# Layer norm and MLP on one core: which of two DMA queues loads the second tile of x

## The chip, the cores and the metric

The kernel runs on one core of a Trainium2 chip. The metric is the device time of one execution in microseconds (us); of several runs the median is given. TensorE is PE in the profile (PEld is its weight load), VectorE is DVE, ScalarE is ACT, GpSimd is POOL, and SyncE is SP. SPq and ACTq are the instructions with which SP and ACT hand a DMA to their queue.

## What is computed

```python
B, S, D, F = 1, 2048, 1024, 3584          # all tensors bf16

def reference(x, w1, b1, w2, b2):
    y = _layernorm(x, axis=-1)            # (x - mean) / sqrt(var + 1e-5), no scale, no shift
    h = _gelu(jnp.einsum("bsd,df->bsf", y, w1) + b1)   # tanh form
    return jnp.einsum("bsf,fd->bsd", h, w2) + b2
```

## The kernel before

**Tiles and blocks.** The 2048 tokens are 16 tiles of 128 (x0, x1, ...), and four tiles make a block of 512. For each block a first product makes 28 rows of h (each 128 features by 512 tokens, eight matmuls over the 1024 input features, L330) and ScalarE applies gelu to each (L350). A second product (L379) takes the block's h times w2, VectorE adds b2 (L390), and SP stores. All weights stay on the chip once loaded, so the loads lie at the start: about 19 MB in the first 60 us, while PE already multiplies.

**The opening.** Block 0 is special, because PE can't wait for four normalised tiles and a whole w1. Tiles 0, 1 and 2 go in as centred but unscaled values (c_sb). Tile 0: ScalarE sums the first half of each row (L400), VectorE the second half (L402), and VectorE subtracts both sums in two pieces (L407). Tiles 1 and 2: `raw_tile` adds the two halves and sums them (L412), then writes 1024*x minus the sum (L416). PE transposes each tile (pe_T, L304) and ScalarE copies the result to yT_sb (L310). The missing scale is multiplied in later, at the first rows of h (L347). Until data are there, PE runs matmuls on a constant (`fill`, L290), 37 of them ahead of tile 0's transposes and two within them.

**The order of PE's work** in the opening is written out by hand. OPEN (L22) lists steps: (0, 0, 2) is tile 0 with the input features 0 to 255, for the first four rows of h (8 matmuls of 128 columns); (1, None) is the transposes of tile 1; and so on:

```python
OPEN = ((0, 0, 2), (1, None), (0, 2, 4), (0, 4, 6), (1, 0, 6), (0, 6, 8), (2, None), (1, 6, 8), (2, 0, 8))
```

PE takes its instructions in this order. A step that isn't ready holds up all steps behind it.

**The pieces of w1** (`w1_chunks`, L111). The first four cover columns 0 to 511 (four rows of h) with 256 input features each, 256 KB apiece. In this text they are called w1 pieces 0 to 3. Piece 0 serves (0, 0, 2), piece 1 (0, 2, 4), piece 2 (0, 4, 6) and the first use of (1, 0, 6) beyond pieces 0 and 1, piece 3 (0, 6, 8). Pieces 4 and 5 cover columns 512 to 767, and four larger pieces follow.

**The order of the loads** (L200 to L220) is the order in which SP and ACT issue them. Each issue is a `dma_start` in the program of the engine whose queue it uses, by way of the helper `dma` (L177, recorded at L178). Tiles 0 and 1 are loaded in halves of 512 columns (128 KB each): the first half by SP, the second by ACT. Then SP alone issues w1 pieces 0, 1, 2, tile 2, piece 3, tile 3, pieces 4 and 5, b1, the rest of w1, block 1 of x, w2, b2 and the last blocks of x. After its two issues ACT runs the table load for gelu (L399) and the sum for tile 0 (L400).

**Waits.** Every DMA has a semaphore of its own. L400 waits for the first half of tile 0, L402 for its second half, L412 for both halves of tile 1 (L421) or for tile 2 (L424). The first matmul that uses a w1 piece waits for that piece, and pe_T waits for the centred tile.

VectorE's other work in the opening (bn_stats of the tiles at L231 for the scale, and the normalisation of tile 3 at L245) stands in a list by hand as well (L421 to L435). Later VectorE work is placed by a planner with estimated times (L521 to L536); it takes those for loads from the running sum of bytes in `dma` and so doesn't know the queue.

## Time and profile before

| | us |
|---|---|
| median of three runs | 398.07 |
| lowest and highest of them | 397.82, 398.11 |
| the profiled execution | 398.39 |
| span of its trace | 397.2 |
| PE busy in that span | 392.3 (99%) |
| DVE, ACT, POOL busy | 156.6, 82.7, 9.5 |

The span runs from the first instruction to the last; the remaining 1.2 us of the profiled execution lie around it. Each time inside the trace counts from the start of the span. "Busy" for PE includes matmuls that wait in the pipeline. The view of waits lists for how long an engine stood idle and what released it; the chain is followed back from the last instruction to what released each step.

| when each load was issued and when its data were there | queue | issued | landed |
|---|---|---|---|
| x0, first half | SP | 0.79 | 3.5 |
| x0, second half | ACT | 0.78 | 3.7 |
| x1, first half | SP | 1.22 | 4.3 |
| x1, second half | ACT | 1.22 | 4.6 |
| w1 piece 0 | SP | 1.69 | 6.36 |
| w1 piece 1 | SP | 2.16 | 7.28 |
| w1 piece 2 | SP | 2.67 | 7.96 |
| x2 | SP | 3.18 | 8.65 |
| w1 piece 3 | SP | 3.69 | 9.39 |

The issue times are the timeline's, the landings the trace's: a load comes down in 16 parts, each of which is recorded, and has landed with the last.

### The profile page before, as it was taken

The page shows a single profiled execution, that of the slowest core. Times are in us where ns is not written, and L with a number is a line of the kernel's source. Part 1 is how long each engine was busy: PE and PEld are TensorE (multiplying, and loading weights), DVE is VectorE, ACT ScalarE, POOL GpSimd, SP SyncE. Part 2 cuts the span into 40 slices and gives each one's busy share as a digit, 9 for nine tenths or more (in the row PEclk, how much of TensorE's full clock was granted, in tenths as well). Part 3 has the DMA queues.
Part 4 walks back from the last instruction along what each step waited for, and adds up shares of the span by engine and source line. Part 5 has one row for each costly group of instructions (what it writes and reads, how often), then busy time and mean ns, then how long its engine had stood idle before and what let it go on. Part 6 is the DMA issues. An engine that isn't in the chain of part 4 may idle for free.

```text
span 397.2 us, 4608 instructions
## 1 busy us (share of the span) xinstructions
PE 392.3 (99%) x1968; PEld 187.9 (47%) x2003; DVE 156.6 (39%) x341; ACT 82.7 (21%) x125; POOL 9.5 (2%) x25
## 2 busy tenths in 40 slices
PE   8999999999999999999999999999999999999998
PEld 8844444444444444444444444444444444444445
DVE  4957889988999405988100000001100000001011
ACT  4264430000134442000024433100003334400000
POOL 0201100011000100000000000000000000000000
DMA  8999940000000000000000000000000000000000
GB/s 257 353 386 386 387 164 15 26 26 16 26 1 2 0 0 2 27 15 26 26 15 0 0 2 0 11 17 26 15 26 13 2 0 0 2 13 26 15 26 26
DMA packets 17357, 23.62 MB, mean 59 GB/s; under 512 B 1082, under 2 KB 9786, under 8 KB 17338
## 3 DMA queue, kind: packets, MB, share of 16 engines
q1 hardware_dynamic: 17050, 23.08, 16.7%
q8 instruction: 15, 0.25, 0.3%
q10 hardware_dynamic: 288, 0.26, 0.2%
q14 instruction: 4, 0.03, 0.0%
HBM read 19.14 MB, written 4.19 MB: 59 GB/s over the span
## 4 chain that ended last, share of the span: by engine, by line
PE 97%; DMA 1%; issue 1%; SPq 0%; DVE 0%
PE ps L379 49%; PE ps L330 48%; DMA w_sb<-in_w_dram 1%; SPq L178 0%; PE ps L304 0%; DVE o_sb L390 0%
## 5 line engine op out<-in xcount | busy, mean ns | idle before, releaser
L330 PE MATMUL ps<-yT_sb,w_sb 128*128 128x512 bf16 (+2 forms) x989 | 193.9, 355 | 1.2
L379 PE MATMUL ps<-w_sb,hT_sb 128*128 128x512 bf16 (+2 forms) x908 | 193.3, 373 | 0.8
L330 PEld LDWEIGHTS ps<-yT_sb,w_sb 128*128 128x128 bf16 x1008 | 92.5, 98 | 101.4 <-DMA w_sb<-in_w_dram 0.6
L379 PEld LDWEIGHTS ps<-w_sb,hT_sb 128*128 128x128 bf16 x924 | 89.2, 98 | 104.5
L350 ACT ACTIVATE hT_sb<-ps,b_sb 128x512 bf16<-128x512 f32 x112 | 76.2, 688 | 255.9 <-PE ps L330 231.8
L390 DVE TENSOR_TENSOR o_sb<-ps,b_sb 128x512 bf16<-128x512 f32 (+2 forms) x33 | 22.3, 675 | 198.9 <-PE ps L379 198.8
L277 DVE STREAM_TRANSPOSE yT_sb<-x_sb 32x256 bf16<-32x256 bf16 x192 | 83.7, 436 | 21.6 <-PE ps L330 18.6
L231 DVE BATCH_NORM_STATS2 st_sb<-x_sb 128x6 f32<-128x512 bf16 x32 | 20.9, 668 | 0.1
L347 DVE TENSOR_TENSOR ps<-ps,rbc_sb 128x384 f32<-128x384 f32 x28 | 15.2, 563 | 9.4 <-PE ps L330 9.0
L235 POOL TENSOR_TENSOR rstd_sb<-mv_sb,nhalf 128x1 f32<-128x1 f32 x16 | 8.7, 549 | 124.2 <-DVE mv_sb L238 124.1
L245 DVE TENSOR_SCALAR x_sb<-x_sb,mv_sb,rstd_sb 128x1024 bf16<-128x1024 bf16 x13 | 7.1, 545 | 2.8 <-POOL rstd_sb L235 2.0
L310 ACT COPY yT_sb<-ps 128x384 bf16<-128x384 bf16 (+2 forms) x10 | 4.5, 504 | 6.8 <-PE ps L304 6.8
L290 PE MATMUL ps<-const-bfloat16-1.0 128*128 128x128 bf16 x39 | 4.5, 310 | 0.8 <-PEq L565 0.8
L290 PEld LDWEIGHTS ps<-const-bfloat16-1.0 128*128 128x128 bf16 x39 | 4.1, 145 | 0.8 <-issue 0.8
L238 DVE BATCH_NORM_AGGREGATE mv_sb<-st_sb 128x2 f32<-128x15 f32 x16 | 3.5, 217 | 0.8
L304 PE MATMUL ps<-ident,c_sb 128*128 128x128 bf16 x24 | 2.4, 249 | 0.1
L402 DVE TENSOR_SCALAR_CACHE_REDUCE junk_d<-x_sb 128x512 bf16<-128x512 bf16 x1 | 0.7, 686 | 3.7 <-DMA x_sb<-in_x_dram 3.7
L304 PEld LDWEIGHTS ps<-ident,c_sb 128*128 128x128 bf16 x24 | 1.8, 111 | 0.3 <-issue 0.3
L412 DVE SCALAR_TENSOR_TENSOR junk_d<-x_sb 128x512 bf16<-128x512 bf16 x2 | 1.4, 688 | 1.1 <-DMA x_sb<-in_x_dram 1.1
L399 ACT ACT_TABLE_LOAD x1 | 1.3, 1283 | 1.7 <-PEq L565 1.7
L446 DVE STREAM_TRANSPOSE rbc_sb<-rs_sb 32x96 f32<-32x96 f32 x4 | 1.1, 270 | 0.1
L416 DVE TENSOR_SCALAR c_sb<-x_sb,sum_sb 128x1024 bf16<-128x1024 bf16 x2 | 1.0, 487 | 0.1
(22 smaller groups left out, 6.8 us busy)
## 6 DMA issues: line engine op xcount, KB each, us to landing
w_sb<-in_w_dram SPq DMA_DIRECT2D x4, 1792.0 KB, 18.5
w_sb<-in_w_dram SPq DMA_DIRECT2D x2, 2048.0 KB, 14.4
out_dram<-o_sb SPq DMA_DIRECT2D x31, 128.0 KB, 1.7
x_sb<-in_x_dram SPq DMA_DIRECT2D x3, 1024.0 KB, 14.5
w_sb<-in_w_dram SPq DMA_DIRECT2D x6, 256.0 KB, 5.5
w_sb<-in_w_dram SPq DMA_DIRECT2D x1, 1024.0 KB, 9.3
x_sb<-in_x_dram SPq DMA_DIRECT2D x2, 256.0 KB, 5.7
w_sb<-in_w_dram SPq DMA_DIRECT2D x1, 512.0 KB, 6.4
```

The source lines that it names most:

```text
L231: return (lambda e, i=i, h=h: e.bn_stats(st_sb[:, i, 6 * h:6 * (h + 1)], x_sb[:, i, h * HC:(h + 1) * HC]), [x_ev.get(i, f"x{i}_{h}")], f"s ...
L235: pool.op(lambda e, i=i: e.tensor_tensor(out=rstd_sb[:, i:i + 1], in0=mv_sb[:, i, 1:2], in1=nhalf[:, i:i + 1], op=ALU.pow), waits=[f"mv{i} ...
L245: return (lambda e, i=i: e.tensor_scalar(out=x_sb[:, i, :], in0=x_sb[:, i, :], scalar1=mv_sb[:, i, 0:1], scalar2=rstd_sb[:, i:i + 1], op0= ...
L277: res.append((lambda e, src=src, dst=dst: e.transpose(out=dst, in_=src), waits, (f"tr{i}" if lastop else None), 0.47))
L290: pe.op(lambda e: e.matmul(ps[:, 0, 0:P], lhsT=one, rhs=one, start=True, stop=True), waits=[gate] if gate else [])
L304: pe.op(lambda e, j=j, o=(j - j0) * P: e.transpose(out=bap[:, o:o + P], in_=src[:, j * P:(j + 1) * P], identity=ident[:, :]), waits=waits, ...
L310: act.op(lambda e, dst=dst, psrc=psrc: e.copy(out=dst, in_=psrc), waits=[f"tp{i}_{j0}"], sig=f"te{i}_{j0}")
L330: pe.op(lambda e, b=b, r=r, dt=dt, n0=n0, n1=n1, bank=bank: e.matmul(ps[:, bank, n0:n1], lhsT=w1_sb[:, dt, r * P:(r + 1) * P], rhs=yT_sb[: ...
L347: crit.append((est[sig], (lambda e, bank=bank: e.tensor_tensor(out=ps[:, bank, 0:n], in0=ps[:, bank, 0:n], in1=rb, op=ALU.mult), [sig, "rb ...
L350: act.op(lambda e, r=r, bank=bank: e.activation(out=hT_sb[:, r, :], in_=ps[:, bank, :], func=ACT.Gelu_apprx_tanh, bias=b1_sb[:, r:r + 1], ...
L379: pe.op(lambda e, st=st, ft=ft, c0=c0, c1=c1, bank=bank: e.matmul(ps[:, bank, 0:c1 - c0], lhsT=hT_sb[:, ft, st * P:(st + 1) * P], rhs=w2_s ...
L390: crit.append((est[sig], (lambda e, ob=ob, c0=c0, c1=c1, bank=bank: e.tensor_tensor(out=o_sb[:, ob, c0:c1], in0=ps[:, bank, 0:c1 - c0], in ...
```

## The change

The loop that loads the first two tiles takes SP's queue for the first half of tile 0 alone. The first half of tile 1 goes to ACT's queue.

```diff
         for i in range(2):
-            for h, q in enumerate((sp, act)):
+            for h, q in enumerate((sp if i == 0 else act, act)):
                 dma(x_sb[:, i, h * HC:(h + 1) * HC], xf[i * P:(i + 1) * P, h * HC:(h + 1) * HC],
                     f"x{i}_{h}", P * HC * 2, q)
         for ci in range(3):
             load_w1(ci)
```

SP's program then begins with the first half of x0, w1 pieces 0, 1, 2, x2, and so on. ACT's begins with the second half of x0, the first half of x1, the second half of x1, the table load. No transfer, wait, semaphore or computation is added or removed.

## The prediction

> **What bounds the kernel now.** I read the page's busy line first, then the chain in order of time, then the waits of the first 20 us, then the timeline from 3.5 to 8 us.

> ```profile
> PE 392.3 (99%) x1968; PEld 187.9 (47%) x2003; DVE 156.6 (39%) x341; ACT 82.7 (21%) x125; POOL 9.5 (2%) x25
> ...
> PE 97%; DMA 1%; issue 1%; SPq 0%; DVE 0%
> ```

> PE is the bound: the chain of what ended last is PE for 97% of the span, and all else on it lies in the first 8 us and in the tail. The opening of the chain in order of time (start, length, what):

> ```profile
> 0.79 0.38 SPq L178
> 1.16 0.06 issue
> 1.22 0.42 SPq L178
> 1.64 0.05 issue
> 1.69 0.43 SPq L178
> 2.12 0.04 issue
> 2.16 0.47 SPq L178
> 2.63 0.04 issue
> 2.67 5.29 DMA w_sb<-in_w_dram
> 7.96 0.05 issue
> 8.00 2.41 PE ps L330 x40
> ```

> The reader is to see that the start is four issues of SP's queue (x0's half, x1's half, w1 pieces 0 and 1), then the flight of w1 piece 2 from its issue at 2.67 to 7.96, and that from 8.00 on PE waits for nothing. The change takes one issue (1.22 to 1.64) out of that row. The waits say how much PE lost to w1 in all (total, times, longest):

> ```profile
> PEld ps L330 <- DMA w_sb<-in_w_dram: 0.6, 2, 0.4
> ```

> And the timeline shows where, with what stands between (start, length; in brackets the idle time before):

> ```profile
> 3.57 0.63 ACT L400 ACTIVATE junk_a<-x_sb 128x512 bf16<-128x512 bf16 x1 [0.58 <-DMA x_sb<-in_x_dram]
> ...
> 5.20 0.68 DVE L412 SCALAR_TENSOR_TENSOR junk_d<-x_sb 128x512 bf16<-128x512 bf16 x1
> ...
> 5.92 0.49 DVE L416 TENSOR_SCALAR c_sb<-x_sb,sum_sb 128x1024 bf16<-128x1024 bf16 x1
> ...
> 6.41 0.47 PEld L330 LDWEIGHTS ps<-yT_sb,w_sb 128*128 128x128 bf16 x8 [0.41 <-DMA w_sb<-in_w_dram]
> ...
> 6.83 0.49 PEld L304 LDWEIGHTS ps<-ident,c_sb 128*128 128x128 bf16 x8
> ...
> 7.32 0.45 PEld L330 LDWEIGHTS ps<-yT_sb,w_sb 128*128 128x128 bf16 x8
> ...
> 8.00 2.23 PEld L330 LDWEIGHTS ps<-yT_sb,w_sb 128*128 128x128 bf16 x40 [0.23 <-DMA w_sb<-in_w_dram]
> ```

> PE waited 0.41 us for piece 0 (to 6.41) and 0.23 us for piece 2 (7.77 to 8.00). Between them it did tile 0 with piece 0, tile 1's transposes, and tile 0 with piece 1. So the whole stake is 0.41 + 0.23 = **0.64 us**, 0.16% of the span. Nothing done to these loads can gain more on PE's path.

> **The change part by part.**

> *SP's queue loses one issue.* SP's issues start 0.43 to 0.51 us apart, so all from piece 0 on are issued about 0.47 us earlier (piece 0 at 1.22, piece 2 at 2.2). An earlier issue helps only if the transfer was waiting for it. It wasn't: the first packet on SP's queue starts at 1.81, 1.03 us after its issue, and in the stretches from 2 us on the 16 DMA engines are 93%, 95%, 107% busy (2 to 4, 4 to 5, 5 to 6 us). Piece 2 was issued at 2.67, while by 4.6 us only 0.47 MB of the 1.05 MB up to its end had moved on that queue. The bytes are what is late, and up to the end of piece 2 they are the same: x0, x1 and three pieces, 1.31 MB, before and after. So I cost the earlier issue itself at zero. If the engines were not full, it would be worth up to the 0.47 us.

> *The order of bytes.* Where both queues have work, they move about alike: from 3.6 to 4.1 us the answer on DMA gives 0.07 MB for SP's and 0.07 MB for ACT's queue; from 2.6 to 3.1 us 0.09 and 0.10. [...]

> *x1 lands later.* ACT's queue carries 384 KB instead of 256 KB. It needed from 2.4 to 4.2 us for 0.26 MB, 0.13 to 0.16 MB per us beside SP's queue, so the third half takes 0.8 to 1.0 us more, and x1 lands at 4.6 + 0.8 to 1.0 = 5.4 to 5.6 instead of 4.6. I take 5.5. Before, L412 started at 5.20, when VectorE was done with tile 0, so x1 had 0.6 us to spare; now L412 starts at 5.5, 0.3 late. From its start to the end of L416 are 6.41 - 5.20 = 1.21 us, so tile 1 is centred at 6.71. PE's transposes of it stood at 6.83, so they can now start at 6.73. Behind L412 on VectorE stand bn_stats of tile 0 (until 7.61); tile 2's L412 waited 1.07 us for x2 until 8.68, which absorbs 0.3.

> *w1 piece 0* lands earlier or not at all earlier. By bytes it ends where it did: 384 KB of SP's queue beside 384 KB of ACT's. But its landing at 6.36 is that of two late parts out of 16: fourteen had landed by 5.37. The same two-part lag, 0.9 to 1.1 us, is in pieces 1 and 2 (fourteen of piece 2 by 6.88, the last at 7.96). It starts with w1: on SP's queue two packets at 3.72 and 3.74 took 0.67 and 0.62 us, where the usual one takes 0.05; these are among the first packets of w1. [...] The lag then shrinks by something between 0 and 1.1 us. I take about 0.2: nearer to zero, since x1's own last parts were 0.3 late at the time of the stall, so a stall seems to hold the other queue partly too.

> *The sum.* PE reaches (0, 0, 2) at 6.0 at the earliest and needs 0.45 us, so it is at tile 1's transposes by 6.71 if piece 0 lands by 6.2. Transposes from 6.73, step (0, 2, 4) from 7.22 (before: 7.32), and (0, 4, 6) from 7.67 if piece 2 is there. Tile 1 alone thus limits the gain to 8.00 - 7.67 = 0.33. With piece 2 at 7.75 the step starts at 7.8, and the gain is **0.2 us**. It stays: piece 3 landed at 9.39 and is asked for at 9.75 - 0.2 = 9.55; tile 2 is centred at 9.89 and asked for at 10.19 - 0.2 = 9.99; tile 3 is normalised at 13.22 and asked for at 13.90 - 0.2. The profiled execution of 398.39 becomes 398.2, and the median, which lies 0.3 below that execution, 398.07 - 0.2 = 397.9.

> *ACT's queue gains one issue* of 0.41 to 0.46 us ahead of the table load. That starts at 1.70 + 0.48 = 2.18 and ends 1.28 later at 3.46. L400 waited 0.58 us for x0 and started at 3.57, so 0.11 us of cover is left: cost zero. Without that cover each 0.1 us would first eat the 0.25 us between the end of L400's sum (4.29) and L407 (4.54), then the 0.41 us at PE.

> *x0* has 128 KB of each queue ahead of anything else, as before. Bounds: 0 to 0.3 us later, if the first w1 packets stall its last parts; PE's 0.41 us cover it.

> **The rivals.**

> *Hidden anyway.* Same bytes, same two late parts, piece 2 at 7.96: PE starts (0, 4, 6) at 8.00 and the time is 398.07, give or take 0.15 (the spread of the runs before). For it: the busy DMA rows. Against it: the lag begins at a place that the change moves.

> *x1 too late (slower).* The price is one for one beyond a point: PE's three steps after centring need 0.96 us, so tile 1 centred after 7.02, L412 after 5.81, x1 landing after about 5.8. At the slowest rate seen (0.28 MB per us for both queues from 3.6 to 4.1, half of it ACT's) x1 lands at 5.55; a stall of 0.65 us on top makes it 6.2, a loss of 0.4: 398.5. If ACT's queue gets a third of the engines' work, the 256 KB of x1 take 2.5 us from 3.2 on, 6.1 with the landing; with a stall 6.7, a loss of 0.9: 399.0. Against it: the even shares in the rows.

> *PE's clock step comes later (slower).* PE's matmuls of 128 columns start 107 ns apart up to 5.95 and 56 ns apart from 6.5 on, although the granted clock reads 1.00 throughout. If a longer gap before tile 0's transposes (now 0.3 us, 4.72 to 5.04) moved the step behind 6.5, each such matmul would cost 0.05 us more; the 64 up to 10.4 us cost at most 3.3, half of them 1.6: 399.7. It decides only if x0 is late. [...]

> *Lag gone wholly and x1 on time.* Gain up to 0.64: 397.4.

> **How the numbers follow.** Forecast with a gain of 0.05 to 0.33 us (397.7 to 398.0): 0.42. Hidden anyway (397.9 to 398.2): 0.30. x1 too late: 0.16, a third of it beyond 0.8 us. Clock: 0.05. More than 0.33 gained: 0.07. The predicted time is 397.9. The range from 397.4 (the whole stake) to 398.9 (x1 late with a stall) leaves out the clock and the worst of x1. A change of 0.2%, 0.8 us, is about what a measurement of this kernel can tell from no change; the whole stake is below it. Faster by more needs something that I don't see: 0.05. Slower by more is the clock and the worst third of x1, with a little for surprises: 0.13. Within: 0.82.

> **What would show it.** The timeline after should have SP's piece 0 at 1.22 and ACT's table load at about 2.2, L400 still at 3.57, tile 1's L412 at 5.4 to 5.6 with a wait for x_sb ahead of it, tile 1's transposes at about 6.75 and step (0, 4, 6) at 7.7 to 7.9. The late parts of piece 0 should land before 6.2. I am wrong if L412 starts after 5.8, if L400 starts late, if piece 2 lands after 8.0, or if PE's 107 ns steps reach past 6.5.

## The result

| | before | after |
|---|---|---|
| median of 12 runs, us | 398.06 | 399.19 |
| lowest and highest | 397.78, 398.57 | 398.65, 401.64 |
| the profiled execution | 398.39 | 401.64 |
| its span | 397.2 | 400.4 |

The changed kernel is slower: the ratio of the runs is 1.0044, 95% interval 1.0031 to 1.0056. Its runs form two groups, seven from 398.65 to 399.30 and five from 400.66 to 401.64; the profiled execution is of the upper one. The ratio is larger than that of the medians (1.0028) because the upper group is five in twelve.

The chain of what ended last, from the trace of after (start, length, what):

```profile
1.70 5.98 DMA x_sb<-in_x_dram
7.67 0.03 issue
7.70 0.02 DVEq L74
7.72 0.06 issue
7.78 0.71 DVE junk_d L412 x2
8.49 0.02 issue
8.51 0.50 DVE c_sb L416
9.01 0.05 issue
9.05 1.03 PE ps L304 x8
10.09 3.54 PE ps L330 x48
```

Before, this stretch was SP's issues and the flight of w1 piece 2. Now it is the flight of the second half of x1, ACT's third load, from its issue at 1.70 to 7.67, and then VectorE's centring of tile 1. The timeline of PE's weight loads (PEld) shows what PE did meanwhile (in brackets the idle time before):

```profile
5.72 0.46 PEld L330 LDWEIGHTS ps<-yT_sb,w_sb 128*128 128x128 bf16 x8 [0.16 <-issue]
9.05 0.77 PEld L304 LDWEIGHTS ps<-ident,c_sb 128*128 128x128 bf16 x8 [2.87 <-DVE c_sb L416]
9.78 3.68 PEld L330 LDWEIGHTS ps<-yT_sb,w_sb 128*128 128x128 bf16 x48
```

The wait for w1 piece 0 is gone (0.41 us before; the step starts at 5.72 instead of 6.41), and so is that for piece 2. In their place PE waits 2.87 us for tile 1. Tile 1's eight transposes then take 0.77 us where they took 0.49, and the next 48 matmuls 3.68. The stretches of the same trace show why (length, busy times with counts, the granted clock, DMA):

```profile
7.00:8.00 1.00, 0.00 (x0) 0.00 (x0) 0.22 (x1) 0.00 (x0) 0.00 (x0) 1.00 1.08 395
8.00:9.00 1.00, 0.00 (x0) 0.00 (x0) 0.96 (x4) 0.00 (x0) 0.00 (x0) 0.68 1.08 356
9.00:10.00 1.00, 0.95 (x10) 0.95 (x11) 1.00 (x2) 0.30 (x1) 0.00 (x0) 0.50 1.19 313
10.00:11.00 1.00, 1.00 (x12) 1.00 (x11) 0.96 (x4) 0.77 (x2) 0.00 (x0) 0.50 1.20 292
11.00:12.00 1.00, 1.00 (x14) 1.00 (x12) 1.00 (x3) 0.00 (x0) 0.00 (x0) 0.62 1.23 271
```

While PE idles the granted clock falls to 0.50. It stays there until about 11.8, and the matmuls of 128 columns start 107 ns apart instead of 56. The eight transposes and the first 18 of the 48 matmuls pay for it, some 1.3 us in all.

**The books balance at tile 2's transposes.** From their start on no trace shows PE waiting for a load again, so the time at which they start, less that of before (10.24), should be the whole difference of the span. It is, to 0.1 us:

| kernel | x1 landed | tile 1's transposes | tile 2's transposes | less before | span less before |
|---|---|---|---|---|---|
| before | 4.6 | 6.89 | 10.24 | | 397.2 |
| changed, 399.39 us (run below) | 6.74 | 8.12 | 11.25 | 1.0 | 1.0 |
| changed, 400.89 us (run below) | 6.62 | 8.00 | 12.76 | 2.5 | 2.5 |
| changed, 401.64 us | 7.67 | 9.05 | 13.47 | 3.2 | 3.2 |
| changed, 402.05 us (run below) | 7.75 | 9.14 | 13.90 | 3.7 | 3.6 |

### The profile page after: what moved, and what is told of

Read it like the earlier page. It is cut to its first block, busy times and chain, and to the rows that moved or that the text cites. A ratio compares the mean times of both kernels' runs of the same rounds, so it can differ in the third digit from the quotient of the medians.

```text
span 400.4 us, 4643 instructions
## 1 busy us (share of the span) xinstructions
PE 395.0 (99%) x2003; PEld 188.9 (47%) x2003; DVE 156.7 (39%) x341; ACT 82.9 (21%) x125; POOL 9.6 (2%) x25
## 4 chain that ended last, share of the span: by engine, by line
PE 97%; DMA 1%; DVE 0%; ACTq 0%; issue 0%; DVEq 0%
PE ps L330 48%; PE ps L379 48%; DMA x_sb<-in_x_dram 1%; PE ps L304 0%; ACTq L178 0%; DVE junk_d L412 0%; DVE c_sb L416 0%; DVE o_sb L390 0%; DVEq L74 0%
## 5 line engine op out<-in xcount | busy, mean ns | idle before, releaser
L330 PE MATMUL ps<-yT_sb,w_sb 128*128 128x512 bf16 (+2 forms) x1008 | 195.7, 357 | 0.0
L330 PEld LDWEIGHTS ps<-yT_sb,w_sb 128*128 128x128 bf16 x1008 | 93.5, 99 | 100.9 <-issue 0.2
L347 DVE TENSOR_TENSOR ps<-ps,rbc_sb 128x384 f32<-128x384 f32 x28 | 15.3, 564 | 11.0 <-PE ps L330 10.6
L304 PE MATMUL ps<-ident,c_sb 128*128 128x128 bf16 x24 | 2.4, 250 | 2.7 <-DVE c_sb L416 2.7
L304 PEld LDWEIGHTS ps<-ident,c_sb 128*128 128x128 bf16 x24 | 1.7, 112 | 3.2 <-DVE c_sb L416 2.9
L412 DVE SCALAR_TENSOR_TENSOR junk_d<-x_sb 128x512 bf16<-128x512 bf16 x2 | 1.4, 684 | 2.6 <-DMA x_sb<-in_x_dram 2.6
L416 DVE TENSOR_SCALAR c_sb<-x_sb,sum_sb 128x1024 bf16<-128x1024 bf16 x2 | 1.0, 486 | 0.1
## 6 DMA issues: line engine op xcount, KB each, us to landing
w_sb<-in_w_dram SPq DMA_DIRECT2D x2, 2048.0 KB, 14.4
```

Source lines behind the costliest of these rows:

```text
L304: pe.op(lambda e, j=j, o=(j - j0) * P: e.transpose(out=bap[:, o:o + P], in_=src[:, j * P:(j + 1) * P], identity=ident[:, :]), waits=waits, ...
L330: pe.op(lambda e, b=b, r=r, dt=dt, n0=n0, n1=n1, bank=bank: e.matmul(ps[:, bank, n0:n1], lhsT=w1_sb[:, dt, r * P:(r + 1) * P], rhs=yT_sb[: ...
L347: crit.append((est[sig], (lambda e, bank=bank: e.tensor_tensor(out=ps[:, bank, 0:n], in0=ps[:, bank, 0:n], in1=rb, op=ALU.mult), [sig, "rb ...
```

## The experiments

My theory after the result had three parts: tile 1 is late because its second half is third on ACT's queue beside w1; PE idles for it (2.87 us in the profile); and where PE idles long, the clock halves (0.50 from 8.36 us on there). The rivals were that the early start of w1 does the harm, and that the upper group has another cause. All experiments are edits of the load order (L200), of PE's order by hand, or matmuls put into PE's gap. The fences show each edit in short: new lines alone, where they replace the loop of L200, and the rest of the order in a comment. `half(i, h, q)` is the `dma` of one half of a tile.

**One part at a time.** First, tile 1 entirely on SP's queue, ahead of w1:

```diff
+  half(0, 0, sp); half(0, 1, act); half(1, 0, sp); half(1, 1, sp)   # then w1 pieces 0, 1, 2
```

> Theory (third place): tile 1 is late because its second half is third on ACT's queue and shares the DMA engines with w1 all the way. Here both halves of tile 1 follow tile 0's half on SP's queue, ahead of w1, and ACT's queue has one load. Tile 1 should land by 4.8, L412 start within 0.1 of 5.2, PE run its steps as before: 397.6 to 398.4 us, no row with a clock below 1. Rival (w1 early): what hurts is that w1's first piece moves; here it moves back by one place, so it also expects the time of before. Rival (number of loads on one queue): with four loads of the opening on SP's queue in a row, one of them is late; then L412 starts after 6 and the time is over 398.6.

Measured: median 398.29 against 398.01 (ratio 1.0007, 0.9998 to 1.0016). Tile 1 landed at 5.29, not by 4.8: one of its parts came at 3.94 and fourteen only by 5.20. L412 started at 5.39, PE's transposes of it at 6.67, and no loss stands clear of the noise. The lateness that the third case feared is there, but small: it costs nothing here.

Then third place on ACT's queue alone, with SP's queue as before. The spare load is work that the kernel doesn't need:

```diff
+  half(0, 0, sp); half(1, 0, sp); half(0, 1, act)
+  dma(spare[:, :], xf[0:P, 0:HC], "spare", P * HC * 2, act)
+  half(1, 1, act)                                       # then w1 pieces 0, 1, 2 on SP
```

> SP's queue is as in the kernel before (x0's half, x1's half, w1). ACT's queue gets one more load of 128 KB between its two, into a tile that nobody reads, so tile 1's second half is third there. Theory (third place): tile 1 is late again, L412 starts at 6.3 to 7.8, PE idles ahead of tile 1's transposes, 398.6 to 401.6 us as in the changed kernel. Rival (w1 early): w1 piece 0 is behind x1's half on SP as before, so tile 1 lands by 5.6, L412 starts by 5.7, and the time is within 0.4 of 398.1.

Measured: 398.77 (1.0030, 1.0011 to 1.0049), two of ten runs above 400.9. Tile 1 landed at 5.96, between the two expectations: third place costs most of the loss, but not all of the lateness. (The spare load adds 128 KB to what moves in the opening, so it isn't third place alone.)

And w1 piece 0 early alone:

```diff
+  half(0, 0, sp); load_w1(0); half(1, 0, sp); half(0, 1, act); half(1, 1, act)
+  load_w1(1); load_w1(2)
```

> Only w1 piece 0 moves ahead of tile 1's first half on SP's queue; that half stays on SP, and ACT's queue is as before. Theory (third place): tile 1's second half lands at about 4.7, its first half behind 384 KB on SP's queue at 5.3 to 6.0; L412 starts at 5.4 to 6.1, tile 1 is centred at 6.6 to 7.3, and the time is 397.8 to 398.5. Rival (w1 early): the early w1 packets slow both queues, tile 1 lands after 6.4, and the time is over 398.6 as in the changed kernel.

Measured: 398.01 (1.0001, 0.9992 to 1.0011). The halves landed at 4.97 (ACT) and 5.43 (SP), L412 started at 5.45. w1 first doesn't harm by itself, so this rival falls.

**Why x1 comes later than its bytes say.** Where ACT's queue carries x1 beside w1 in these traces, x1's last half never lands with an equal amount of w1, but with twice as much. In the changed kernel x1 (256 KB) lands with w1 piece 1, that is 512 KB of w1: 7.67 and 7.87. With the spare load the last 128 KB of ACT's queue land with the 256 KB of piece 0: 5.96 and 5.87. With w1 first, again 128 KB (4.97) with piece 0 (4.96). Beside x1's other half, in the kernel before, it was one to one (4.6 and 4.3). A half of x has one row of 1 KB for each partition; a piece of w1 has two. So I formed the theory ("turns" in the expectations) that the queues' shares go with the bytes that a load has for one partition. Two kernels tell it apart from a matter of the bytes on ACT's queue: one gives x1 rows of 2 KB, the other gives w1 one row of 1 KB for each partition.

```diff
+  half(0, 0, sp); half(0, 1, act); load_x_tile(1, act)   # tile 1 as one load, rows of 2 KB
```

> The changed kernel, but tile 1 is one load on ACT's queue with rows of 2 KB in place of two loads with rows of 1 KB. The bytes on each queue and their order are the same. [...] With 2 KB in a row tile 1 should move at the pace of w1, and land together with w1 piece 0, at 5.0 to 5.7; L412 starts at 5.2 to 5.8, and the time is 397.8 to 398.4. Rival (bytes on ACT's queue): it lands with w1 piece 1 as in the changed kernel, at 6.2 to 6.9, 398.6 us or more.

Measured: 398.12 against 398.05 (1.0001, 0.9991 to 1.0010), ten runs from 397.94 to 398.32, no upper group. Tile 1 landed at 5.37 with w1 piece 0 (5.53); L412 started at 5.39.

```diff
-    w1_chunks = [(j, j + 2, 0, 512) for j in range(0, DT, 2)] + ...
+    w1_chunks = [(j, j + 1, 0, 512) for j in range(4)] + [(4, 6, 0, 512), (6, 8, 0, 512)] + ...
```

> The changed kernel, but w1 pieces 0 and 1 are two loads each, of 128 KB with one row of 1 KB for each partition, as x's halves have. Bytes and order are the same; SP issues two more loads, 0.45 us each. Theory (turns): the two queues now move alike, x1's second half lands beside 256 KB of w1 instead of 512 KB, at 5.0 to 5.7, L412 starts at 5.2 to 5.8, and the time is 397.8 to 398.6. Rival (bytes on ACT's queue, or SP's queue served first): it lands at 6.2 to 6.9 as before, 398.6 us or more.

Measured: 398.68 against 398.05 (1.0010, 1.0001 to 1.0019). Tile 1 landed at 5.73 with the second of the four quarter loads (5.48), after 256 KB of w1 and not after 512 KB. That is the theory's case. The time missed its expectation by a little: L412 started at 5.83, tile 2 landed at 8.77, and runs reached 399.22. Tile 1's second half is third on ACT's queue here too, so third place with even shares costs about 0.1%, against 0.3% for the changed kernel beside it (ratio 1.0030, 1.0012 to 1.0049; its runs are below).

The view of DMA shows the shares directly. The columns are packets, MB, and time as a share of 16 engines; q1 is SP's queue, q10 ACT's. The changed kernel from 3.6 to 5.6 us, w1 beside x1:

```profile
q1 hardware_dynamic: 362, 0.35, 64.6%
q10 hardware_dynamic: 211, 0.19, 28.7%
```

Tile 1 as one load with rows of 2 KB, from 3.6 to 4.8:

```profile
q1 hardware_dynamic: 214, 0.21, 50.0%
q10 hardware_dynamic: 115, 0.22, 48.1%
```

w1 in loads with one row of 1 KB for each partition, from 3.6 to 4.6:

```profile
q1 hardware_dynamic: 165, 0.15, 46.1%
q10 hardware_dynamic: 173, 0.16, 45.4%
```

ACT's queue moves 0.54 of what SP's does in the first, and as much in the other two. In these kernels the share went with the bytes of a load, and not with its rows or the bytes that a queue has to move; how the engines come to that share is not shown. All these loads cover 128 partitions, so the bytes for one partition and the size of the whole load (128 or 256 KB) can't be told apart.

**The clock.** The changed kernel with 40 matmuls on a constant in the gap:

```diff
+            if st == OPEN[0]:
+                for _ in range(40):
+                    pe.op(lambda e: e.matmul(ps[:, 6, 0:P], lhsT=one, rhs=one, start=True, stop=True))
```

> The changed kernel with 40 more matmuls on a constant (into a bank that nobody reads before its next start) between PE's step (0, 0, 2) and tile 1's transposes; at 0.056 us each they take 2.2 us, 6.2 to 8.4. Tile 1's loads are as late as in the changed kernel. Theory (late tile 1 plus halved clock): the clock stays at 1.00, matmuls of 128 columns stay 0.056 us apart from 6.5 on, the slow group of the changed kernel's runs (400.7 to 401.6) disappears, and all runs lie between 398.4 and 399.8. Rival (the slow group is only a later tile 1): the two groups stay, with runs above 400.6.

Measured: 399.93 (1.0047, 1.0032 to 1.0062), four runs from 399.64 to 400.32. The upper group is gone, with the clock at 1.00, but the median is 0.1 over the expectation, and three of the four runs are. In its trace tile 1 landed at 6.59 and was centred at 7.91, while the 40 matmuls held PE until tile 1's transposes at 8.78. They cost more than they saved. Four runs are also few to show that a group is gone, so the next two make the gap long in every run: tile 1 behind w1 piece 3 on SP's queue, without and with matmuls in the gap.

```diff
+  half(0, 0, sp); half(0, 1, act)                        # then w1 0, 1, 2, x2, w1 3
+  half(1, 0, sp); half(1, 1, sp)                         # then x3, w1 4, 5
```

> Tile 1's halves are moved far back on SP's queue, behind w1 piece 3, to make PE's idle time long in every run. Tile 1 should land at about 9.4, be centred at 10.6, and PE idle from 6.2 to 10.6, 4.4 us. Theory (halved clock after a long idle time): in all runs the matmuls behind the gap start 0.107 us apart for a while, the clock reads 0.5 there, and the kernel loses the shift of tile 1's transposes (10.6 against 6.8: 3.8 us) and another 1.2 to 3.4 us: 403 to 405.3 us. Rival (no clock effect, only lateness): 401.5 to 402.2 us.

> The kernel with tile 1 very late, and 62 matmuls on a constant in PE's gap ahead of tile 1's transposes: 3.5 us at 0.056 us each, 6.2 to 9.7, so that about 0.9 us stay idle. They compute nothing that is used. Theory (halved clock after a long idle time): the clock stays at 1.00, and the kernel loses only the lateness, 401.5 to 402.2 us, which is 1.2 to 3.4 us better than the same kernel without the matmuls. Rival (no clock effect): both take the same time within 0.3 us.

Measured: 403.81 without, 401.53 with the 62 matmuls (all four runs from 403.32 to 405.06, and from 401.46 to 401.97). The stretches without:

```profile
6.00:10.00 4.00, 0.45 (x8) 0.28 (x5) 0.99 (x3) 0.56 (x2) 0.00 (x0) 0.70 1.09 351
10.00:11.00 1.00, 0.75 (x8) 0.75 (x9) 1.00 (x3) 0.10 (x1) 0.00 (x0) 0.50 1.21 290
11.00:12.00 1.00, 1.00 (x12) 1.00 (x11) 0.99 (x3) 0.97 (x2) 0.00 (x0) 0.50 1.23 285
```

And with:

```profile
6.00:10.00 4.00, 4.00 (x70) 3.90 (x67) 0.58 (x1) 0.54 (x2) 0.00 (x0) 1.00 1.09 364
10.00:11.00 1.00, 0.38 (x8) 0.31 (x7) 0.96 (x4) 0.00 (x0) 0.00 (x0) 1.00 1.25 299
11.00:12.00 1.00, 1.00 (x22) 1.00 (x20) 1.00 (x3) 0.87 (x2) 0.00 (x0) 1.00 1.13 289
```

At a clock of 0.50 PE starts a matmul of 128 columns every 107 ns, and at 1.00 every 56 ns. (The counts 12 and 22 include those that only reach into a stretch.) Matmuls that nobody needs made the kernel 2.3 us faster, although tile 1's transposes started later with them in the profiles (10.70 against 10.25). The halved clock after an idle stretch is shown: 0.50 where PE's weight loads had idled for 3.97 us, and 1.00 where the matmuls left 0.79 us of that. Its price is about 2 us in these two profiles: the 39 matmuls from 10.25 to 14.4 start 51 ns further apart, and the profiled times differ by 1.5 us (403.50 and 401.97) in spite of the later start.

**The two groups.** The changed kernel again:

> The changed kernel once more, beside the next two on one chip. The runs of the changed kernel fell into two groups (398.65 to 399.3, and 400.66 to 401.64). Theory (late tile 1, and halved clock where it is latest): a profile of the lower group has tile 1's second half landing at 6.2 to 6.9 and no clock below 1; of the upper one at 7.4 or later with clock rows of 0.5. Median 398.7 to 399.4. Rival (the groups have to do with something else, such as the end of the kernel): tile 1 lands at the same time in both.

> One more look at the changed kernel, for a profile of the lower group of its runs. Theory: with a time below 399.5 tile 1's second half lands at 6.2 to 6.9, PE idles 1.0 to 1.7 us ahead of tile 1's transposes, the matmuls behind them start 0.056 us apart, and the clock reads 1.00. With a time above 400.6 it lands at 7.4 or later, PE idles over 2.3 us, and the clock reads 0.5 behind.

> The same look again, with the same two cases: below 399.5 us tile 1's second half lands at 6.2 to 6.9 and the clock stays at 1.00; above 400.6 it lands at 7.4 or later and the clock reads 0.5 behind PE's gap.

Measured: ten runs with a median of 399.11, two of them at 400.75 and 402.05, the latter profiled; then 399.39 and 400.89. Part of my account fell here. In these last two, tile 1 landed at 6.74 and 6.62 and PE's weight loads idled for 1.68 and 1.87 us, almost alike, and yet only one lost the clock. The execution of 399.39 us:

```profile
7.00:8.00 1.00, 0.00 (x0) 0.00 (x0) 0.96 (x4) 0.00 (x0) 0.00 (x0) 1.00 1.04 374
8.00:9.00 1.00, 0.88 (x16) 0.89 (x17) 1.00 (x3) 0.45 (x1) 0.00 (x0) 1.00 1.09 358
9.00:10.00 1.00, 1.00 (x22) 1.00 (x20) 0.96 (x4) 0.62 (x2) 0.00 (x0) 1.00 1.17 320
```

That of 400.89 us:

```profile
7.00:8.00 1.00, 0.00 (x1) 0.01 (x1) 0.96 (x4) 0.00 (x0) 0.00 (x0) 1.00 1.09 390
8.00:9.00 1.00, 1.00 (x15) 1.00 (x16) 1.00 (x2) 0.57 (x2) 0.00 (x0) 0.79 1.09 328
9.00:10.00 1.00, 1.00 (x12) 1.00 (x11) 0.96 (x4) 0.51 (x2) 0.00 (x0) 0.50 1.19 293
```

The 48 matmuls behind tile 1's transposes took 2.84 and 4.47 us: 1.6 us for the clock, most of the 2.1 between the middles of the groups (398.89 and 400.98). So the groups are with and without the halved clock, as I had it. The mean granted clock of each run confirms it: 0.996 in all eight runs of the changed kernel above 400.6 us and in the two upper ones with the spare load, 1.000 in all the others of these two kernels; 3.4 us at half the clock lower the mean over 400 us by 0.4%. But the lateness of tile 1 alone doesn't decide between the groups. It adds on top: 7.67 and 7.75 instead of 6.6 to 6.7 are the two highest profiled times. In these four profiles of the changed kernel idle times of 1.87 us and more went with the halved clock and 1.68 us did not; see the last section.

**A try at a better version.** Tile 1 as one load, and one step of PE moved ahead of its transposes:

```diff
-OPEN = ((0, 0, 2), (1, None), (0, 2, 4), ...
+OPEN = ((0, 0, 2), (0, 2, 4), (1, None), ...
```

> Tile 1 as one load with rows of 2 KB on ACT's queue, and PE's order by hand changed in one place: tile 0 with w1 piece 1 now comes ahead of tile 1's transposes. With the old order PE idled from 6.26 to 6.67 for tile 1 while w1 piece 1 had landed at 6.21. Theory (PE's order makes the wait for tile 1 cost): PE goes on at 6.3 with piece 1, 0.45 us, and reaches tile 1's transposes at 6.7 when they are ready; 0.3 to 0.4 us less than with the old order: 397.6 to 397.8 against 398.0 for the kernel before. Rival (the next wait takes its place, for w1 piece 2, landed 6.9, or tile 2): 397.9 to 398.2.

Measured: 397.96 against 397.95 (1.0001, 0.9992 to 1.0010). The rival holds: PE no longer waits for tile 1's centring, but 0.18 us at 8.18 for ScalarE's copy of it, and in this trace x0 landed at 3.80 and PE's first step began at 6.02, where it was 3.40 and 5.68 with tile 1 as one load and the old order. No version here beats the kernel before.

## Why the prediction was wrong

The forecast of 397.9 and the range up to 398.9 both missed 399.19. It was the rival "x1 too late", with the rival on the clock on top of it in about a third of the runs.

*SP's queue loses one issue.* Piece 0 was issued at 1.22 and landed at 4.87 instead of 6.36 (at 5.00 to 5.57 in the other three profiles), so PE's 0.41 us were there to be had. I had taken 6.2, with even shares and most of the lag; the 0.2 us by which I let the lag shrink was my estimate, and no run shows that term. Its fourteenth part came at 4.84 instead of 5.37, as w1 was issued earlier and got more than its half (0.35 of 0.54 MB from 3.6 to 5.6 us), and the lag behind it shrank from 1.0 to 0.03 (0.6 at most in the others).

*x1 lands later.* This step failed: the sum had x1 at 5.5, and it landed at 6.62 to 7.75. Two terms of it were mis-sized. The first is ACT's rate, which was too high. I took 0.13 to 0.16 MB per us, mostly from stretches in which SP's queue carried x as well, and applied it to stretches in which it carries w1. There the view of DMA shows 0.19 MB in 2 us, and 0.23 in the execution of 399.39 us, 0.10 to 0.12 per us. So the fourteenth part of x1's second half landed at 5.95 to 6.54 in the four profiles. With even shares (w1 in quarter loads) it came at 5.18 and the last at 5.73, near the forecast. The row behind my even shares was this, from 3.6 to 4.1 us of before:

```profile
q1 hardware_dynamic: 70, 0.07, 64.0%
q10 hardware_dynamic: 76, 0.07, 38.1%
```

SP's queue was still finishing its own half of x1 then (4.29), so the row couldn't show ACT's share beside w1.

The second term is the lag of the last parts, which the sum put at nothing for x1: 0.6 to 1.2 us on top. By the rival's rule (one for one beyond a landing at 5.8) the execution of 399.39 us would have lost about 0.2 us without it, and it lost 1.0. That is an estimate; no run takes away the lag alone.

*The rival's price* was right. With a third of the engines' work for ACT's queue I had x1 at 6.1, with a stall at 6.7, and 399.0 us; the one profile of the lower group has x1 at 6.74, with 0.8 us of lag in it, and the group is 398.65 to 399.30. What was wrong was its chance of 0.16, with only a third of that for a loss beyond 0.8 us.

*PE's clock.* I priced it at up to 1.6 us for half of the 64 matmuls and measured 1.6. But I tied it to a late x0 and didn't ask what the gap behind a late x1 would do. The two rivals were not independent: the first brings the second.

*ACT's queue gains one issue.* Right: the table load started at 2.21 (forecast 2.18), and L400 at 3.50, no later than before.

*The lag of two parts* shrank for piece 0, as I had it, but it didn't go away: it came at x1's second half and w1 piece 1. In two of the four profiles of the changed kernel the last of the 16 parts of x1's second half came 1.2 us after the fourteenth, in the other two 0.6 and 0.8; before, x1 had landed by the time the lag began, and it was 0.1. Its origin stays open.

## What to carry to other kernels

Moving a small load to another queue changes not only its place in a row but its share of the engines: two queues didn't split evenly here where one had more bytes for each partition in a load (0.35 against 0.19 MB in 2 us), so read the share from a stretch that holds the same pair of loads. A wait of 2 us that stops TensorE in the opening must be priced twice, once as idle time and once as the chance of a halved clock behind it (here idle times of 1.87 to 3.97 us had it behind them, at a price of 1.3 to 2 us). Where a small load has to share the engines with larger ones, wide rows got it through in time here (tile 1 landed at 5.37, not at 6.62 to 7.75); work put into TensorE's gap kept the clock at 1.00, but paid only where the gap was long (62 matmuls in 4 us; 40 in under 2 us cost more than they saved).

## What the runs showed of the hardware

In these traces the shares of the two DMA queues went with the bytes that each load has for one partition (or, which is the same here, with the size of the load): 1.8 to 1 for 2 KB against 1 KB (0.35 and 0.19 MB from 3.6 to 5.6 us), even for 2 KB against 2 KB (0.21 and 0.22 MB from 3.6 to 4.8) and for 1 KB against 1 KB (0.15 and 0.16 MB from 3.6 to 4.6).
